# Last chunk of an attention stage reordered on TensorE, and place stores spread over two steps

## The chip, the cores and the metric

The kernel runs on one core of a Trainium2 chip. The metric is the device time of one execution in microseconds (us). Four runs of the kernel before took 470.43 to 471.54 us, with a median of 470.91 us.

The engines are named as in the profile: PE is the matrix engine (TensorE), PEld its weight loads, DVE the vector engine, ACT the scalar engine, POOL the GpSimd engine and SP the engine that only issues transfers. SBUF is the on-chip memory, PSUM the eight banks that PE writes its products to.

## The reference

Two blocks follow each other. The first is a linear attention with decay, on `q`, `k`, `v` of shape (4, 8, 768, 64): batch, heads, sequence, head dimension. Within a block of positions it is a masked product, and between blocks a state of 64 by 64 for each batch and head is carried on:

```python
for b in range(nb):
    intra = np.einsum('bhic,bhjc->bhij', qb, kb) * Dmask[None]
    intra = np.einsum('bhij,bhjd->bhid', intra, vb)
    inter = np.einsum('bhid,bhde->bhie', qb * lam_pow[None], kv_state)
    out[:, :, sl] = intra + inter
    kv_state = lam_block[None, :, None, None] * kv_state \
        + np.einsum('bhsd,bhse->bhde', kb * rev_pow[None], vb)
```

Its output, as 3072 tokens of 512 numbers, goes through a mixture of eight experts, each token to the one with the highest logit:

```python
logits = x @ w_gate                              # (3072, 512) @ (512, 8)
expert_idx = np.argmax(logits, axis=1)
...
h = np.maximum(xe @ w1[e], 0.0)                  # w1: (8, 512, 1024)
out[mask] = gate_w[mask, None] * (h @ w2[e])     # w2: (8, 1024, 512)
```

## The kernel before, in words

**Attention.** The sequence is cut into six chunks of 128 positions (n = 0 to 5). One step handles one chunk of two batches, so there are twelve steps, in the order (0; 0,1), (0; 2,3), (1; 0,1) and so on. In the code `cur` is the step's work, `last` the one before and `ahead` the one after. A step of the loop at line 710 does this:

- `leave(last)`: `rows` (lines 313 to 329) turns the finished output of the step before back into rows with matmuls into PSUM banks 4 to 7 (lines 319 and 321). Eight extra columns give the gate logits. ACT copies both out (325, 326) and writes the rows to `xs` in device memory. When the chunk's batches are complete, `choose` picks an expert for each token on DVE.
- `enter(ahead)`: loads for one chunk later are issued on SP; PE transposes q and k (line 207), and ACT and DVE copy them out.
- `attend_states(cur, 0)`, line 265: sixteen small matmuls, 64 by 64, of queries with the carried state, half of what the state gives. They write PSUM banks 6 and 7 (`op`). ACT then copies one element of the second bank to a tile called `fence` (line 273). The matmuls of `attend` that write that bank have to wait for this copy.
- `grow(cur)`, line 294: the state's increment. The last chunk has none.
- `attend(cur)`, line 277: the masked part, 32 matmuls of 128 by 64 into the same two banks.
- `attend_states(cur, 1)`: the other half of the state's part. Then `to_sbuf` (line 286) has ACT copy the two banks to the tiles `xT`, which `rows` reads in the next step, and `update` brings the state up to date.
- `give_places` for a chunk whose experts are chosen: `put` counts with two small matmuls into bank 5 (`rank`, line 375) which place a token takes on its expert's list, and computes its address on DVE (lines 384 to 389, result `slot_i`). One indirect transfer from POOL (line 391) for each batch then writes the tokens' entries to the lists in device memory, `slots`.
- `score(ahead)`, line 242: 32 matmuls of queries with keys for the next step. DVE multiplies them with the decays (line 248).

Chunks 0 to 4 have their places given once for all four batches, the last chunk once for each pair of batches. Chunk 3 is called `early`: when its places are stored, `start_early` (line 688) loads the first 256 places of expert 0 (`list_0a`), and POOL gathers those tokens from `xs` (`fetch`, line 437). After the loop, `turn(passes[0])` (line 466) transposes them on PE. Then come the places of the last chunk, with `leave` between its two pairs.

**Experts.** Eight experts follow in nine passes, since expert 0 is cut in two (0a and 0b). The first two passes multiply directly (lines 476 and 611). The later ones use seven products for eight (lines 552 and 580), for which POOL adds and subtracts blocks of the weights first (lines 513 and 516). Which expert comes first among the others is read back from the counts, so the lists and weights of the first pass after expert 0 are loaded on SP only after all places are stored (lines 413 and 174). Its tokens are gathered on POOL (line 437), partly behind the four sums of its first weights.

**What sets the order.** A planner orders each engine's instructions from estimated durations and readiness, and sets the semaphores. PE's matmuls of the attention stage, of `turn(passes[0])` and the counting matmuls of all but the last pair are pinned: on PE they stay in the order in which the program writes them. Matmuls of the passes, the small DVE work, ACT's copies and POOL's work are free, apart from what they depend on. Each engine then runs its own list strictly in order.

Of the kernel before, what the change touches and what calls it, by code (L numbers as in the profile page):

```python
# [10 lines left out]
F32 = mybir.dt.float32  # L11
# [10 lines left out]
def kernel(  # L22
# [29 lines left out]
    nc = tc.nc  # L52
# [4 lines left out]
    P = 128  # L57
    C = P
    NSTEP = S // C
    HP = H // 2  # L60
# [15 lines left out]
    const = ctx.enter_context(tc.tile_pool(name="const", bufs=1))  # L76
# [41 lines left out]
    nc.vector.memset(ones, 1.0)  # L118
    zeros = const.tile([P, P], F32, name="zeros")
    nc.vector.memset(zeros, 0.0)  # L120
    fence = const.tile([P, 1], F32, name="fence")

    nc.scalar.copy(fence, zeros[:, :1])

    rev = const.tile([P, E], F32, name="rev")
    nc.gpsimd.iota(rev, pattern=[[-1, E]], base=E, channel_multiplier=0,
# [15 lines left out]
    entry = const.tile([P, NSTEP, B, ENTRY], F32, name="entry")  # L142
# [46 lines left out]
    def bank(i, shape, name):  # L189
        return ps.tile(shape, F32, tag=f"bank{i}", name=name)  # L190
# [3 lines left out]
    halves = [slice(0, D), slice(D, P)]  # L194
# [3 lines left out]
    def pin(inst):  # L198
        tc.keep_in_program_order(inst)
# [37 lines left out]
    def score(m, s):  # L237

        shp = [P, HP // 2, 2, C]
        sp = [bank(2 * s + u, shp, f"sp{u}") for u in range(2)]  # L240
        for i, b, u in itertools.product(range(HP // 2), range(2), range(2)):
            pin(nc.tensor.matmul(  # L242
                sp[u][:, i, b, :], lhsT=m.kT[s][halves[u], i, b, :], rhs=m.qT[s][halves[u], i, b, :],
                start=(i == 0 and b == 0), stop=(i == HP // 2 - 1 and b == 1),
                skip_group_check=True))
        mt = work.tile([P, 2, HP // 2, 2, C], F32, tag="mt", name="mt")
        for u in range(2):
            nc.vector.tensor_mul(  # L248
                mt[:, u], sp[u],
                decay[:, u, s * HP // 2:(s + 1) * HP // 2].unsqueeze(2).to_broadcast(shp))  # L250
        m.mt.append(mt)
# [3 lines left out]
    def out_at(m, b, u, hp):  # L255
        return m.op[b][halves[u ^ (hp & 1)], hp, :]

    def attend_states(m, way):

        if way == 0:  # L260
            m.op = [bank(6 + b, [P, HP, C], f"op{b}") for b in range(2)]
        if m.n > 0:
            for hp, b in itertools.product(range(HP), range(2)):
                u = b ^ way
                pin(nc.tensor.matmul(  # L265
                    out_at(m, b, u, hp), lhsT=st[halves[u], m.b + b, hp, :],
                    rhs=m.qsT[hp // 2][halves[u], hp % 2, b, :],
                    start=(way == 0 and hp < 2), stop=(way == 1 and hp >= HP - 2),
                    skip_group_check=True))
        if m.n > 0 and way == 0:  # L270


            nc.scalar.copy(fence[halves[0]], out_at(m, 1, 1, HP - 1)[:, C - 1:])  # L273

    def attend(m):
        for hp, b, u in itertools.product(range(HP), range(2), range(2)):
            pin(nc.tensor.matmul(  # L277
                out_at(m, b, u, hp), lhsT=m.v[:, b, 2 * hp + u, :],
                rhs=m.mt[hp // 2][:, u, hp % 2, b, :],
                start=(m.n == 0 and hp == 0), stop=(m.n == 0 and hp == HP - 1),  # L280
                skip_group_check=True))

    def to_sbuf(m):
# [5 lines left out]
    def grow(m):  # L289

        if m.n < NSTEP - 1:
            m.cp = bank(4, [P, 2, HP, D], "cp")
            for hp, b, u in itertools.product(range(HP), range(2), range(2)):
                pin(nc.tensor.matmul(  # L294
                    m.cp[halves[u], b, hp, :],
                    lhsT=m.kd[hp // 2][:, b, 2 * (hp % 2) + u, :],
                    rhs=m.v[:, b, 2 * hp + u, :],
                    start=(hp == 0 and b == 0), stop=(hp == HP - 1 and b == 1),
                    skip_group_check=True))
# [68 lines left out]
    def put(n, bs, oh, ohc):  # L368


        nb = len(bs)
        shp = list(oh.shape)
        rank = bank(5, shp, "rank")
        for lhs, rhs in ((before, oh), (ones, ohc[:, :shp[1]])):
            mm = nc.tensor.matmul(rank, lhsT=lhs, rhs=rhs, start=(lhs is before),
                                  stop=(lhs is ones))

            if (n, bs[-1]) != (NSTEP - 1, B - 1):
                pin(mm)
        if shp[1] > nb:  # L380
            nc.vector.tensor_copy(had, rank[:, nb, 0:1])
        shp[1] = nb
        place = small.tile(shp, F32, tag="place", name="place")
        nc.vector.tensor_add(place, rank[:, :nb], base[0].unsqueeze(1).to_broadcast(shp))
        nc.vector.tensor_mul(place, place, oh[:, :nb])
        slot = small.tile([P, nb], F32, tag="slot", name="slot")
        nc.vector.reduce_sum(slot, place, axis=AX.X)
        slot_i = small.tile([P, nb], I32, tag="slot_i", name="slot_i")
        nc.vector.tensor_copy(slot_i, slot)  # L389
        for i, b in enumerate(bs):  # L390
            put = nc.gpsimd.indirect_dma_start(  # L391
                out=slots, out_offset=bass.IndirectOffsetOnAxis(ap=slot_i[:, i:i + 1], axis=0),
                in_=entry[:, n, b, :], in_offset=None)

            tc.declare_no_dep(put.ins, group="put", reason="disjoint rows of the lists")
            tc.add_to_no_dep_group("put", put.ins)

    empty = ffn.tile([P, E * R // P, ENTRY], I32, tag="xg", name="empty", bufs=2)
    nc.gpsimd.memset(empty, 0)
# [49 lines left out]
    def evac(i, dst, src):  # L449
        if i % 2:  # L450
            nc.scalar.copy(dst, src)
        else:
            nc.vector.tensor_copy(dst, src)  # L453
# [7 lines left out]
    def turn(m, pin=lambda inst: inst):  # L461
        m.xgT = ffn.tile([P, DC, m.n], F32, tag="xgT", name="xgT", bufs=1)
        for dc in range(DC):
            tp = bank(next(tp_banks), [P, m.n], "tp")
            for t, w in enumerate(m.widths):
                pin(nc.tensor.transpose(tp[:, t * P:t * P + w],  # L466
                                        m.xg[t // 2][:w, t % 2, dc * P:(dc + 1) * P],
                                        ident[:w, :w]))
            evac(dc, m.xgT[:, dc, :], tp)
# [178 lines left out]
    early = groups[NSTEP - 3]  # L648
# [16 lines left out]

    chosen = []

    def give_places(group):
        put(*group)
        if group[:2] == early:  # L670
            start_early()

    def leave(m):
        for b in range(2):
            n, bs = group_of[m.n, m.b + b]
            i = bs.index(m.b + b)
            if i == 0:
                lgs[0] = small.tile([P, len(bs), DC // 2, E], F32, tag="lg", name="lg")
            rows(m, b, lgs[0][:, i])
            if i == len(bs) - 1:  # L680

                chosen.append(choose(n, bs, lgs[0]))

    had = const.tile([P, 1], F32, name="had")
    passes = []
    skip = const.tile([P, 1], F32, name="skip")

    def start_early():

        nc.vector.tensor_scalar(out=skip, in0=had, scalar1=-1.0, scalar2=float(EARLY),  # L690
                                op0=ALU.mult, op1=ALU.add)
        nc.vector.tensor_scalar_max(skip, skip, 0.0)
        base[0] = const.tile([P, E], F32, name="ebase_late")
        nc.vector.tensor_copy(base[0], ebase)
        nc.vector.tensor_add(base[0][:, 0:1], base[0][:, 0:1], skip)
        m = make_pass(0, 0, EARLY, "0a")
        fetch(m, 1 + (NSTEP - 2) * B * C)
        passes.append(m)

    order = [(n, b) for n in range(NSTEP) for b in range(0, B, 2)]  # L700
    cur, last = enter(*order[0]), None
# [4 lines left out]
    for j, u in itertools.product(range(2), range(2)):  # L706
        pin(nc.scalar.dma_start(
            out=back[(u ^ j) * D:((u ^ j) + 1) * D, :, P + j * E:P + (j + 1) * E],
            in_=by_chunk[j, u]))
    for i in range(len(order)):  # L710
        due = chosen.pop() if chosen else None
        if last:
            leave(last)

        ahead = enter(*order[i + 1]) if 0 < i < len(order) - 1 else None
        attend_states(cur, 0)
        grow(cur)
        attend(cur)
        attend_states(cur, 1)
        to_sbuf(cur)  # L720
        if i == 0:
            ahead = enter(*order[1])
        update(cur)
        if i == 0:
            later_decays()

        if due:
            give_places(due)
        if i == 2:
            empty_lists()  # L730
        if ahead:
            for s in range(2):
                score(ahead, s)
        last, cur = cur, ahead
    turn(passes[0], pin)
    give_places(chosen.pop())
    leave(last)
    give_places(chosen.pop())


    cnt = bank(7, [P, E], "cnt")
# [19 lines left out]
                            op=ALU.is_equal)  # L761
# [55 lines left out]
    with tc.If(most > 0):  # L817
        for i in range(E):
            tiles = nc.values_load(beyond[0:1, i:i + 1], min_val=0, max_val=MORE[i])
            with tc.If(tiles > 0):  # L820
# [4 lines left out]
                with tc.For_i(0, tiles, 1) as r:  # L825
                    m = SimpleNamespace(n=P, widths=[P])
# [36 lines left out]
```

## Time and profile before

| | |
|---|---|
| median of four runs | 470.91 us (470.43 to 471.54) |
| the profiled execution | 470.12 us, of which the span is 468.2 us |
| granted TensorE clock in the span | 0.995 |
| attention, steps of the last chunk | about 110 to 131 us |
| first pass of expert 0 (line 476, line 611) | about 128 to 158 us |
| end of the first seven-product pass's gather | about 168 us |

All times inside an execution count from the span's start. A line of the order of time shows start, length, engine, line, operation, output and inputs, shape and count. In brackets stands how long the engine was idle before it and what ended that. PE's matmuls are pipelined: one of 270 ns may start every 37 to 62 ns, so the distance between starts, and not the length, tells the pace. "issue" as a releaser means that the profile shows nothing that the engine waited for.

### The profile page before, as it was taken

To read this page: it belongs to the slowest core of one execution; us is meant where nothing else is said; L and a number is where in the kernel's file an instruction comes from. 1 tells how busy PE (TensorE), PEld (TensorE's weight loads), DVE (VectorE), ACT (ScalarE), POOL (GpSimd) and SP (SyncE) were. 2 spreads that over 40 slices of the span, in tenths; PEclk is the share of its full clock that TensorE was granted. 3 is DMA by queue.
4 is the path that set the end of the run, shared out by engine and by line. 5 is a ranking of instruction groups with operands and counts; after the bars stand their busy time and mean duration, and the time that the engine had idled before them with its cause. 6 is when DMAs were issued, how large, how long until landed. Compare 5 with 4: busy or idle time off the path is not lost.

```text
span 468.2 us, 8613 instructions
## 1 busy us (share of the span) xinstructions
PE 449.5 (96%) x3447; PEld 373.3 (80%) x3447; DVE 222.0 (47%) x495; ACT 125.5 (27%) x323; POOL 246.9 (53%) x190
## 2 busy tenths in 40 slices
PE   5899999999899999999999999999999999999994
PEld 4789899998686667957994898699699689779863
DVE  3646859576550134452345437434524623753421
ACT  3454444554320111212121122113112212211210
POOL 5323636433163949859707951991695497711001
PEclk9999999999999999999999999999999999999998
DMA  9999999999317576060606152351624516001001
GB/s 178 228 259 255 221 245 230 243 264 357 95 48 275 179 262 221 25 251 30 224 1 247 48 203 109 138 202 49 244 92 155 231 34 224 1 20 45 1 18 52
DMA packets 99840, 72.60 MB, mean 155 GB/s; under 512 B 81235, under 2 KB 81239, under 8 KB 99792
## 3 DMA queue, kind: packets, MB, share of 16 engines
q1 hardware_dynamic: 90608, 52.49, 41.3%
q0 software_dynamic: 5008, 13.16, 7.8%
q10 hardware_dynamic: 4176, 6.31, 3.9%
q8 instruction: 29, 0.48, 0.5%
q14 instruction: 19, 0.16, 0.1%
HBM read 58.88 MB, written 13.16 MB: 154 GB/s over the span
## 4 chain that ended last, share of the span: by engine, by line
PE 62%; issue 4%; DMA 4%; POOL 4%; DVE 1%; SPq 0%; POOLq 0%; ACT 0%; DVEq 0%
PE p L552 27%; PE p L580 18%; PE po L611 14%; PE tp L466 3%; DMA w1t<-in_moe_w_dram 2%; POOL slots L391 1%; DMA slots<-entry,slot_i 1%; DMA xg<-xs,list 1%; POOL out_dram L443 1%; POOL s_k L516 1%; POOL w1t L513 1%; POOL s_q L516 1%; SPq L413 0%; DVE h_qsT L499 0%; POOL xg L437 0%
## 5 line engine op out<-in xcount | busy, mean ns | idle before, releaser
L611 PE MATMUL po<-w2t,hT 128*128 128x512 f32 (+5 forms) x224 | 81.0, 597 | 0.0
L437 POOL DMA_INDIRECT xg<-xs,list x24 | 25.8, 1075 | 70.2 <-PE tp L466 64.7
L611 PEld LDWEIGHTS po<-w2t,hT 128*128 128x128 f32 (+5 forms) x224 | 30.6, 162 | 38.2 <-issue 37.9
L563 ACT ACTIVATE hT<-hT 128x408 f32<-128x408 f32 (+4 forms) x56 | 29.5, 527 | 86.7 <-DVE hT L561 86.7
L443 POOL DMA_INDIRECT out_dram<-o,list x24 | 23.7, 989 | 50.9 <-DVE o L617 27.7
L552 PE MATMUL p<-xgT,w1t 128*128 128x204 f32 (+4 forms) x224 | 41.5, 329 | 0.0
L232 POOL TENSOR_TENSOR kd<-k_in,kdec 128x512 f32<-128x512 f32 x20 | 20.4, 1043 | 37.4 <-PE cp L294 23.5
L552 PEld LDWEIGHTS p<-xgT,w1t 128*128 128x128 f32 x224 | 37.6, 190 | 1.2 <-issue 0.9
L391 POOL DMA_INDIRECT slots<-entry,slot_i x24 | 23.3, 972 | 24.9 <-DVE slot_i L389 19.1
L248 DVE TENSOR_TENSOR mt<-sp,decay 128x512 f32<-128x512 f32 x48 | 29.8, 683 | 11.6 <-PE sp L242 11.4
L592 DVE SCALAR_TENSOR_TENSOR o<-p,list,o 128x256 f32<-128x256 f32 x28 | 13.6, 484 | 32.9 <-PE p L580 17.0
L580 PE MATMUL p<-w2t,hT 128*128 128x256 f32 x112 | 26.8, 382 | 0.0
L580 PEld LDWEIGHTS p<-w2t,hT 128*128 128x128 f32 x112 | 21.1, 190 | 7.0 <-issue 4.5
L242 PE MATMUL sp<-qT,kT 64*128 64x128 f32 x384 | 24.9, 279 | 0.0
L242 PEld LDWEIGHTS sp<-qT,kT 64*128 64x128 f32 x384 | 22.6, 188 | 1.8 <-issue 1.0
L277 PE MATMUL op<-mt,v_in 128*64 128x128 f32 x384 | 23.5, 274 | 0.2 <-ACT fence L273 0.2
L561 DVE TENSOR_TENSOR hT<-p,u_qsT 128x408 f32<-128x408 f32 (+4 forms) x28 | 15.7, 561 | 15.8 <-PE p L552 15.8
L466 PEld LDWEIGHTS tp<-ident,xg 128*128 128x128 f32 (+3 forms) x112 | 13.3, 140 | 11.9 <-issue 3.4
L476 PE MATMUL ph<-xgT,w1t 128*128 128x256 f32 (+1 forms) x128 | 22.5, 333 | 0.0
L286 ACT COPY xT<-op 128x512 f32<-128x512 f32 x24 | 12.9, 589 | 35.0 <-PE op L265 29.1
L277 PEld LDWEIGHTS op<-mt,v_in 128*64 128x64 f32 x384 | 20.7, 137 | 0.9 <-ACT fence L273 0.5
L466 PE MATMUL tp<-ident,xg 128*128 128x128 f32 (+3 forms) x112 | 18.6, 274 | 2.8 <-DVE xgT L453 1.4
(163 smaller groups left out, 934.5 us busy)
## 6 DMA issues: line engine op xcount, KB each, us to landing
w1t<-in_moe_w_dram SPq DMA_DIRECT2D x8, 2048.0 KB, 8.4
w2t<-in_moe_w_dram SPq DMA_DIRECT2D x8, 2048.0 KB, 8.5
v_in<-in_v_dram SPq DMA_DIRECT2D x12, 512.0 KB, 8.5
xs<-x ACTq DMA_DIRECT2D x24, 256.0 KB, 5.0
q_in<-in_q_dram SPq DMA_DIRECT2D x11, 512.0 KB, 8.2
k_in<-in_k_dram SPq DMA_DIRECT2D x11, 512.0 KB, 8.5
q_in<-in_q_dram SPq DMA_DIRECT2D x2, 256.0 KB, 3.8
k_in<-in_k_dram SPq DMA_DIRECT2D x2, 256.0 KB, 5.3
```

The costliest lines, as they stand in the source:

```text
L242: pin(nc.tensor.matmul(sp[u][:, i, b, :], lhsT=m.kT[s][halves[u], i, b, :], rhs=m.qT[s][halves[u], i, b, :], start=(i == 0 and b == 0), st ...
L248: nc.vector.tensor_mul(mt[:, u], sp[u], decay[:, u, s * HP // 2:(s + 1) * HP // 2].unsqueeze(2).to_broadcast(shp))
L277: pin(nc.tensor.matmul(out_at(m, b, u, hp), lhsT=m.v[:, b, 2 * hp + u, :], rhs=m.mt[hp // 2][:, u, hp % 2, b, :], start=(m.n == 0 and hp = ...
L391: put = nc.gpsimd.indirect_dma_start(out=slots, out_offset=bass.IndirectOffsetOnAxis(ap=slot_i[:, i:i + 1], axis=0), in_=entry[:, n, b, :] ...
L437: nc.gpsimd.indirect_dma_start(out=dst, out_offset=None, in_=xs[:rows, :], in_offset=bass.IndirectOffsetOnAxis(ap=idx, axis=0))
L443: put = nc.gpsimd.indirect_dma_start(out=out, out_offset=bass.IndirectOffsetOnAxis(ap=idx, axis=0), in_=src, in_offset=None, bounds_check= ...
L466: pin(nc.tensor.transpose(tp[:, t * P:t * P + w], m.xg[t // 2][:w, t % 2, dc * P:(dc + 1) * P], ident[:w, :w]))
L476: nc.tensor.matmul(ph, lhsT=w1t[:, dc, fc * P:(fc + 1) * P], rhs=m.xgT[:, dc, :], start=(dc == 0), stop=(dc == DC - 1))
L552: nc.tensor.matmul(p[:, i, :], lhsT=lhs[:, dc, (c + i) * P:(c + i + 1) * P], rhs=rhs[:, dc, :], start=(dc == 0), stop=(dc == DH - 1))
L563: nc.scalar.activation(outs[i][k], outs[i][k], ACT.Relu)
L580: nc.tensor.matmul(p, lhsT=lhs[:, fc, :], rhs=rhs[:, fc, :], start=(fc == 0), stop=(fc == FC // 2 - 1))
L611: nc.tensor.matmul(po[part], lhsT=m.hT[:, fc, t * P:t * P + w], rhs=w2t[:, fc, :], start=(i < k), stop=(i >= FC - k), skip_group_check=True)
```

## The change

For the last chunk (n = 5) alone, a step does the masked part `attend` first and then the states' first part, and the fence copy now reads two elements on all partitions. The scores of the next step come next, or in the very last step `turn(passes[0])`, and only then the states' second part. In all steps with states the second part takes batch 1 before batch 0. The stores of a chunk's places are no longer issued at once: `put` returns a function, `store_places` issues two of them in the step and two in the next one, and `start_early` comes when the early chunk's last store is issued.

```diff
-    fence = const.tile([P, 1], F32, name="fence")
-    nc.scalar.copy(fence, zeros[:, :1])
+    fence = const.tile([P, 2], F32, name="fence")
+    nc.scalar.copy(fence, zeros[:, :2])
...
+    def attend_begin(m):
+        m.op = [bank(6 + b, [P, HP, C], f"op{b}") for b in range(2)]
+
     def attend_states(m, way):
-        if way == 0:
-            m.op = [bank(6 + b, [P, HP, C], f"op{b}") for b in range(2)]
         if m.n > 0:
-            for hp, b in itertools.product(range(HP), range(2)):
+            for hp, b in itertools.product(range(HP), (0, 1) if way == 0 else (1, 0)):
                 u = b ^ way
                 pin(nc.tensor.matmul(
                     out_at(m, b, u, hp), lhsT=st[halves[u], m.b + b, hp, :],
                     rhs=m.qsT[hp // 2][halves[u], hp % 2, b, :],
-                    start=(way == 0 and hp < 2), stop=(way == 1 and hp >= HP - 2),
+                    start=(way == 0 and hp < 2 and m.n < NSTEP - 1),
+                    stop=(way == 1 and hp >= HP - 2),
                     skip_group_check=True))
         if m.n > 0 and way == 0:
-            nc.scalar.copy(fence[halves[0]], out_at(m, 1, 1, HP - 1)[:, C - 1:])
+            if m.n < NSTEP - 1:
+                nc.scalar.copy(fence[halves[0], :1], out_at(m, 1, 1, HP - 1)[:, C - 1:])
+            else:
+                nc.scalar.copy(fence, m.op[1][:, 0:HP:HP - 1, C - 1])
 
     def attend(m):
...
-                start=(m.n == 0 and hp == 0), stop=(m.n == 0 and hp == HP - 1),
+                start=(m.n in (0, NSTEP - 1) and hp == 0), stop=(m.n == 0 and hp == HP - 1),
...
-        for i, b in enumerate(bs):
+        def store(i):
             put = nc.gpsimd.indirect_dma_start(
                 out=slots, out_offset=bass.IndirectOffsetOnAxis(ap=slot_i[:, i:i + 1], axis=0),
-                in_=entry[:, n, b, :], in_offset=None)
+                in_=entry[:, n, bs[i], :], in_offset=None)
...
+        return store
...
+    waiting = []
+
+    def store_places():
+        for group, store, i in waiting:
+            for j in range(i, min(i + 2, len(group[1]))):
+                store(j)
+        done = [group for group, _, i in waiting if i + 2 >= len(group[1])]
+        waiting[:] = [(group, store, i + 2) for group, store, i in waiting
+                      if i + 2 < len(group[1])]
+        if any(group[:2] == early for group in done):
+            start_early()
+
     def give_places(group):
-        put(*group)
-        if group[:2] == early:
-            start_early()
+        waiting.append((group, put(*group), 0))
...
-        attend_states(cur, 0)
-        grow(cur)
-        attend(cur)
+        attend_begin(cur)
+        if cur.n < NSTEP - 1:
+            attend_states(cur, 0)
+            grow(cur)
+            attend(cur)
+        else:
+            attend(cur)
+            attend_states(cur, 0)
+            if ahead:
+                for s in range(2):
+                    score(ahead, s)
+            else:
+                turn(passes[0], pin)
         attend_states(cur, 1)
         to_sbuf(cur)
...
         if due:
             give_places(due)
+        store_places()
         if i == 2:
             empty_lists()
-        if ahead:
+        if ahead and cur.n < NSTEP - 1:
             for s in range(2):
                 score(ahead, s)
         last, cur = cur, ahead
-    turn(passes[0], pin)
     give_places(chosen.pop())
+    store_places()
     leave(last)
     give_places(chosen.pop())
+    store_places()
```

## The prediction

> **What bounds the kernel now.** I read the page's first table first, and then busy time by stage, for the stretch that the change rewrites and what follows:
>
> ```profile
> PE 449.5 (96%) x3447; PEld 373.3 (80%) x3447; DVE 222.0 (47%) x495; ACT 125.5 (27%) x323; POOL 246.9 (53%) x190
> ```
>
> ```profile
> 113.80:128.90 15.10, 13.00 (x190) 10.47 (x190) 8.16 (x34) 5.75 (x19) 3.06 (x4) 1.00 0.46 132
> 128.90:168.30 39.40, 39.10 (x192) 28.44 (x189) 9.03 (x45) 6.14 (x21) 24.67 (x20) 1.00 0.51 165
> 168.30:300.00 131.70, 131.70 (x644) 102.23 (x645) 59.75 (x105) 26.92 (x52) 86.61 (x51) 1.00 0.42 151
> ```
>
> PE is busy 96% of the 468.2 us span, so idle time of PE is what can move the end. In the stages the first pair is window and length, the next number PE's busy time. PE idles 2.10 us in the last chunk's two steps (113.8 to 128.9), 0.3 us in the 39 us after them, and nothing from 168.3 to 300. What PE loses before 168.3 the end loses. The third view is the order of time on all engines inside that stretch (start, length, engine, line):
>
> ```profile
> 114.39 0.44 PE L277 MATMUL op<-mt,v_in 128*64 128x128 f32 x4
> 115.05 1.75 PE L277 MATMUL op<-mt,v_in 128*64 128x128 f32 x28 [0.21 <-ACT fence L273]
> 117.44 1.08 ACT L286 COPY xT<-op 128x512 f32<-128x512 f32 x2 [2.45 <-PE op L265]
> 122.81 2.08 PE L277 MATMUL op<-mt,v_in 128*64 128x128 f32 x32
> 125.42 0.19 PE L375 MATMUL rank<-oh,before 128*128 128x32 bf16 x1
> 125.67 0.19 DVE L384 TENSOR_TENSOR place<-rank,ebase_late 128x32 f32<-128x32 f32 x1 [1.41 <-PE rank L375]
> 126.48 0.33 PE L466 MATMUL tp<-ident,xg 128*128 128x128 f32 x1 [0.84 <-DMA xg<-xs,list_0a]
> 127.48 0.42 DVE L453 COPY xgT<-tp 128x256 f32<-128x256 f32 x1 [1.54 <-PE tp L466]
> 127.82 0.18 DVE L385 TENSOR_TENSOR place<-place,oh 128x32 f32<-128x32 f32 x1
> 128.25 0.17 DVE L389 CAST slot_i<-slot 128x4 int32<-128x4 f32 x1
> 128.70 1.00 POOL L391 DMA_INDIRECT slots<-entry,slot_i  x1 [4.63 <-DVE slot_i L389]
> 128.94 0.48 PE L319 MATMUL tx<-back,xT 128*128 128x136 f32 x2
> ```
>
> To be seen: the fence costs something once, at 115.05; the first token tiles (xg of list_0a) land only at 126.48 and PE waits for them; chunk 4's list addresses (slot_i) are late because DVE stands at the evacuation of those tiles before it goes on with line 385. The chain that ended last says why that is not idle detail:
>
> ```profile
> 132.54 2.68 DMA slots<-entry,slot_i
> ...
> 137.59 2.08 DMA slots<-entry,slot_i
> ...
> 142.23 8.99 DMA w1t<-in_moe_w_dram
> ...
> 163.81 4.44 DMA xg<-xs,list
> 168.25 0.04 issue
> 168.29 1.17 PE tp L466 x6
> ```
>
> Eight stores of places run back to back on POOL from 128.70, 1.26 us apart (0.96 and 0.30 idle); the last one lands at 139.67; then come list loads, the second expert's w1 (landed 151.22), four sums of 2.35 us on POOL, two scatters, a gather, and PE, which is done with its own work at 168.02 (167.64 + 0.38), waits for that gather to 168.29. Two paths of the same length meet there: PE's own and the chain that begins with slot_i of chunk 4. The later one sets the end.
>
> **Part by part.**
>
> *Step for (5, batches 0 and 1).* Removed: the fence wait. States to scores took 5.51 us (113.80 to 119.31); without the wait the same work is 0.60 + 2.01 + 0.60 + 1.99 = 5.20 (attend from 122.81 to 124.82), so 0.31 is gained. Lost: the cover of the xT copies. Now 1.99 us of scores stand between the states' second part and the rows of line 319, which need xT; the two copies (1.08 us) hide in them. With the scores ahead of the second part, the rows follow it at once and wait for the first copy: 0.12 from the last start to ACT (117.32 to 117.44), 0.59 for one copy (row of line 286: 589 ns), 0.05 to PE, 0.76 in all. Net +0.45 us. The new fence (two elements on 128 partitions, one ACT copy like the old one at 158 ns) hides under the scores, which need nothing of it; were that cover gone it would cost the old 0.3.
>
> *Step for (5, batches 2 and 3).* Before, states, attend, states and rank run from 121.87 to 125.5. After: +0.45 at the start, the wait for the banks of the rows as before, attend and the first states to 125.15, then the turn of the first pass. Its data do not come earlier: the four stores of group 3 carry no new wait between them on POOL (no other POOL work lies between 109.93 and 114.73), the list load behind them left at 119.34, the gathers at 121.82 and 123.11. So the 0.45 is absorbed, and PE waits from 125.15 to 126.48, 1.33 us, for what cost it 0.95 before (125.53 to 126.48). The eight transposes with their evacuations last to 128.4, or to 128.8 with two of line 476's matmuls between them as now. Only then come the states' second part (0.60) and the rank of chunk 4: 129.0 to 129.4 instead of 125.42. Behind this rank on PE stand the rank of (5; 0,1) and the rows of (5; 2,3), and both wait: the second rank for the first place (line 384), the rows for xT, again uncovered. They start 0.76 after 129.0 to 129.4, at 129.8 to 130.2 instead of 128.94. PE path: +0.9 to +1.3; if the two matmuls of line 476 (0.42) are not inside the turn they come later, if two or three fill the new gap they give 0.4 to 0.6 back. I take +1.1, bounds +0.6 (the states' second part alone moved behind the gather) and +1.5.
>
> *The chain of places.* From rank to place 0.25 (125.42 to 125.67), from place to slot_i three steps of 0.21, from slot_i to the store 0.45: 1.32 after 129.0 to 129.4 is 130.3 to 130.7, against 128.70. So +1.6 to +2.0, although DVE's stand behind the evacuation (126.0 to 127.8) is gone. All eight stores follow back to back, since the last slot_i (135.34) had half a microsecond in hand and moves with them. Nothing later in the chain has slack before 168.25.
>
> *Stores two and two.* The same 24 stores. Those of groups 0 to 2 move past sd on POOL (for group 0: two at 51.1, two near 60.6 instead of 53.8) and kd of line 232 comes 2.5 us earlier (56.01 now); PE uses that kd at 64.91. Cost 0. If the cover were gone, a store costs POOL 1.26. The small DVE work that starts the early list moves one step later, ahead of base's next use at 125.67: 0. SP has nothing between its loads and the list load at 119.34, so what is moved past it costs nothing.
>
> *Order (1, 0) in the states' second part, in ten steps.* The trace has no such handover, so it is bounded: 0 from the scores' 1.98 us, which stand alike after states (38.47 to 40.46) and after attend (28.48 to 30.46); at best the longest matmul of line 265 (0.32 us) a step, 3.2 in all; at worst the 0.17 of idle that the weight loads show at a change of form, +1.7. I take 0, as the scores' row is the same handover with another predecessor.
>
> *Sum.* At 168.29: the larger of PE +1.1 less its 0.27 of wait, and the chain +1.85. End +1.85, on the profiled execution's 470.12 (span 468.2 and 1.9 around it): 471.97. That execution lies 0.79 under the median 470.91 of the runs; against the median it is 472.7 (rounded down from 472.76), which I give.
>
> **Two rules weighed.** PE already waits 0.84 us for xg at 126.48 in the row above. The Trainium skill, page "DMA: Bandwidth & Descriptors", section "Rules for kernel authors", advises to issue a DMA early and wait for it late, with compute in between; the change puts that wait ahead of 0.60 us of ready states. By that rule alone the sum would be +0.6.
> Weight loads idle 0.17 us at each change of form (125.42, "issue"). The page "TensorEngine Tiling (Array Packing)", section "Key Properties", says that changing the tiling mode drains TensorE. By it the last step's one further change of form would add 0.17; the row gives the same figure, but the starts of the scores show none of it on PE, so the sum goes without it.
>
> **Rivals.**
> *Filled gap.* The order on PE that is not pinned is the planner's. If it sees the late gather of 163.81 and puts matmuls of line 611 ahead of the transposes, the chain's delay hides behind them and PE's +1.1 remains: 471.2, against the median 472.0. For it: two of line 611 already stand between them at 169.39. Against: in the trace six transposes come first, though PE had to wait. 0.18.
> *Cancelled.* The early places land sooner: the row of their DMAs has 2.1 to 7.3 us to landing, the fourth early one took about 5.5 (113.77 to 119.3). At 2.1 the gather would be in by 123, the turn would begin at 125.15, rank of chunk 4 fall at 127.7, the store at 129.0: +0.3, or 471.2 against the median. Against: the change touches none of the traffic there. 0.08.
> *Faster.* The handover of the states' second part to the scores: in ten steps, gaining g each. It outweighs +1.85 from g = 0.19 on, and from 0.28 the gain passes 0.2% (0.94 us, about what a measurement of this kernel can tell from no change); at its bound of 0.32 the time is 470.9 + 1.85 - 3.2 = 469.6. Against it stands the equal 1.98. 0.10.
> *Worse.* The planner lets a sum (2.35 us) of POOL stand ahead of the gather at 163.81: +4.2, 475.1. For: from 151.36 to 166.0 POOL is never idle for more than 0.3 us, so nothing there would absorb it. 0.12.
>
> **How the numbers follow.** My forecast (chain late, +1.6 to +2.0, 472.5 to 472.9) has 0.52, filled gap 0.18, worse 0.12, faster 0.10, cancelled 0.08. Slower by over 0.2%: 0.52, the worse case's 0.12 and 0.10 of the filled gap (its bounds are 0.6 and 1.5, the line is 0.94): 0.74. Same: the other 0.08 of the filled gap and the cancelled case's 0.08: 0.16. Faster: 0.10. The range reaches down to 470.7, through the filled gap and most of the cancelled case, and up to 474.4, part of the way to the worse case; left out are the faster case and most of the worse one, 0.2.
>
> **What would show it.** Right: PE waits about 1.3 us for xg before line 466; the rank of chunk 4 behind these transposes, near 129.2; its first store near 130.5; a wait of 0.6 to 0.8 us of line 319 for xT near 119.1; a wait for xg near 168 to 170 of over 1 us. Wrong: the first store of chunk 4 before 129.5, or matmuls of line 611 ahead of the transposes at 168, or a different total of PE between 25 and 113.8, where I expect no change.

## The result, and the profile after

The changed kernel takes 473.44 us in the median of 52 runs (469.4 to 476.0), the kernel before, run beside it, 471.88 us in 78 (468.04 to 475.52). The ratio is 1.0032, with a 95% interval from 1.002 to 1.0044: slower by about 1.5 us. The profiled execution of the changed kernel took 474.02 us with a span of 472.2 us, 4.0 us longer than the span profiled before. A part of those 4.0 us belongs to that one execution, as will be seen. The page's first table shows PE busy for 2.8 us longer with the same 3447 matmuls:

```profile
PE 452.3 (96%) x3447; PEld 375.9 (80%) x3447; DVE 221.1 (47%) x495; ACT 125.7 (27%) x323; POOL 247.3 (52%) x190
```

The stages tell where. In these lines stand the window, its length, the busy time and count of PE, PEld, DVE, ACT and POOL, the granted clock of TensorE, the DMA share and GB/s:

```profile
113.80:128.90 15.10, 10.87 (x164) 8.88 (x160) 6.41 (x28) 4.19 (x15) 2.59 (x3) 0.96 0.41 116
128.90:168.30 39.40, 39.19 (x178) 27.60 (x178) 9.71 (x50) 6.74 (x21) 23.34 (x19) 0.93 0.45 151
...
124.00:126.00 2.00, 0.66 (x18) 0.42 (x16) 0.11 (x1) 0.16 (x1) 0.00 (x0) 1.00 0.82 272
126.00:128.00 2.00, 0.33 (x1) 0.14 (x1) 0.00 (x0) 0.00 (x0) 0.00 (x0) 0.95 0.20 80
128.00:130.00 2.00, 1.83 (x7) 1.14 (x7) 0.63 (x2) 0.37 (x1) 0.00 (x0) 0.50 0.00 0
130.00:132.00 2.00, 2.00 (x21) 1.44 (x21) 0.73 (x5) 1.06 (x3) 0.00 (x0) 0.50 0.00 0
132.00:134.00 2.00, 2.00 (x9) 1.57 (x7) 0.85 (x6) 0.39 (x1) 0.81 (x1) 0.50 0.00 0
134.00:136.00 2.00, 2.00 (x16) 2.00 (x15) 0.00 (x0) 0.94 (x5) 1.39 (x3) 0.84 0.02 1
```

Two things are to be seen. PE is busy 10.87 us of the last chunk's 15.10, where it was 13.00: the wait is there, and larger than forecast. And behind the wait TensorE's granted clock is halved for about 6.8 us, from 127.8 to 134.6, where the profile before shows 1.00. The order of time has both, with what they did to the places:

```profile
113.56 1.97 PE L282 MATMUL op<-mt,v_in 128*64 128x128 f32 x32
...
119.41 0.50 PE L324 MATMUL tx<-back,xT 128*128 128x136 f32 x2 [0.70 <-ACT xT L291]
...
124.00 0.67 PE L266 MATMUL op<-qsT,st 64*64 64x128 f32 x16
...
126.83 0.33 PE L474 MATMUL tp<-ident,xg 128*128 128x128 f32 x1 [2.16 <-DMA xg<-xs,list_0a]
128.08 2.11 PE L474 MATMUL tp<-ident,xg 128*128 128x128 f32 x7 [0.92 <-DMA xg<-xs,list_0a]
130.11 1.13 PE L266 MATMUL op<-qsT,st 64*64 64x128 f32 x16
131.18 0.21 PE L380 MATMUL rank<-oh,before 128*128 128x32 bf16 x1
...
132.74 0.17 DVE L394 CAST slot_i<-slot 128x4 int32<-128x4 f32 x1
133.19 1.00 POOL L396 DMA_INDIRECT slots<-entry,slot_i  x1 [9.50 <-DVE slot L392]
```

(The changed kernel's lines are shifted: 266 was 265, 282 was 277, 324 was 319, 380 was 375, 396 was 391, 474 was 466.) No fence wait is left at line 282. The rows of line 324 wait 0.70 us for xT. PE stands 2.16 us for the first token tile and 0.92 for the second, with one transpose between them. The sixteen state matmuls of line 266 that took 0.67 us at 124.00 take 1.13 at 130.11, which is the halved clock. The rank of chunk 4 comes at 131.18 instead of 125.42 and the first of the last eight stores at 133.19 instead of 128.70. The chain that ended last runs through the token gather and then stays on PE but for some 2 us on DVE from 136.87 (start, length, what):

```profile
122.73 5.30 DMA xg<-xs,list_0a
128.03 0.04 issue
128.08 0.49 PE tp L474
...
165.02 7.38 PE ph L484 x62
172.40 1.17 PE tp L474 x8
```

At 172.40 there is no wait for the gather, as there was one of 0.27 us at 168.29 before. In this execution PE itself, delayed by wait and clock, reached that point as late as the chain of places did.

### The profile page after: what moved, and what is told of

Its sections match the earlier page's. It is cut to its first block, busy times and chain, and to the rows that moved or that the text cites. A ratio compares the mean times of both kernels' runs of the same rounds, so it can differ in the third digit from the quotient of the medians.

```text
span 472.2 us, 8624 instructions
## 1 busy us (share of the span) xinstructions
PE 452.3 (96%) x3447; PEld 375.9 (80%) x3447; DVE 221.1 (47%) x495; ACT 125.7 (27%) x323; POOL 247.3 (52%) x190
## 4 chain that ended last, share of the span: by engine, by line
PE 70%; issue 2%; DVE 1%; DMA 1%; POOL 1%; POOLq 0%; ACT 0%
PE p L560 27%; PE p L588 18%; PE po L619 17%; PE ph L484 4%; PE tp L474 3%; DMA xg<-xs,list_0a 1%; POOL slots L396 0%; DVE h_qsT L507 0%; PE tx L324 0%; PE tx L326 0%; PE op L266 0%; DVE hT L569 0%; DVE xgT L461 0%; POOLq L848 0%; ACT hT L571 0%
## 5 line engine op out<-in xcount | busy, mean ns | idle before, releaser
L484 PE MATMUL ph<-xgT,w1t 128*128 128x256 f32 (+1 forms) x128 | 23.6, 342 | 0.0
```

Source lines behind the costliest of these rows:

```text
L484: nc.tensor.matmul(ph, lhsT=w1t[:, dc, fc * P:(fc + 1) * P], rhs=m.xgT[:, dc, :], start=(dc == 0), stop=(dc == DC - 1))
```

## The experiments

Two theories stood at the start. *Order*: the last step's order delays the rank, so the places, so the gather near 168, by about 1.9 us at full clock. *Clock*: PE's wait in the turn lets TensorE's granted clock fall to half, and that is the cost. A third question was whether the other parts cost anything. Twelve measurements were made in three comparisons, each with runs of the kernel before beside it. The median of the kernel before was 471.86 us (35 runs) in the first, 477.5 (30) in the second and 471.64 (35) in the third. In the second, attention ran 4 to 5 us later than in the profiles shown so far; what follows from that is told with it.

**The changed kernel with the last step as it was.**

```diff
-        if cur.n < NSTEP - 1:
+        cur.masked_first = cur.n == NSTEP - 1 and ahead is not None
+        if not cur.masked_first:
...
-            if ahead:
-                for s in range(2):
-                    score(ahead, s)
-            else:
-                turn(passes[0], pin)
+            for s in range(2):
+                score(ahead, s)
...
+    turn(passes[0], pin)
     give_places(chosen.pop())
```

> The changed kernel, but its very last step in the old order: states, masked part, states, rank of chunk 4, then the turn of the first pass. Everything else of the change stays (masked part first and scores between in the step for (5; 0,1), stores two and two, batch 1 before batch 0). Clock theory (PE idles some 3.4 us before the turn, its granted clock then halves for about 6 us): the wait for xg falls to 0.5 to 1.0 us, the granted clock of the span stays at 0.995 or more, the chunk-4 stores start within 0.3 us of the 128.7 of the kernel before, ratio to before 0.998 to 1.001. Order theory (chunk 4's places and the rows stand behind the gather, whatever the clock): the same ratio, 0.998 to 1.001. Rival that the loss is in the other parts (scores between, stores, batch order): ratio stays near 1.003.

Measured: 471.28 us, ratio 0.9986 (0.9957 to 1.0014). The loss is gone with the last step's order. The order of time of this kernel:

```profile
125.32 0.19 PE L380 MATMUL rank<-oh,before 128*128 128x32 bf16 x1
...
126.76 0.33 PE L474 MATMUL tp<-ident,xg 128*128 128x128 f32 x1 [1.23 <-DMA xg<-xs,list_0a]
...
129.06 1.00 POOL L396 DMA_INDIRECT slots<-entry,slot_i  x1 [4.68 <-DVE slot_i L394]
```

The rank is back at 125.32 and the first store at 129.06. It still holds the uncovered xT copy (0.71 us at line 324), the stores two and two and the order (1, 0): together they cost nothing that shows. Its span of 469.6 us has a halved clock too, from about 127.5 to 130.9.

**The last step's order alone, in the kernel before.**

```diff
-        attend_states(cur, 0)
-        grow(cur)
-        attend(cur)
+        attend_begin(cur)
+        cur.masked_first = ahead is None and i > 0
...
+            attend(cur)
+            attend_states(cur, 0)
+            turn(passes[0], pin)
         attend_states(cur, 1)
...
-    turn(passes[0], pin)
```

> The kernel before with the last step alone reordered as in the change: masked part, states' first part, turn of the first pass, states' second part (batch 1 first, in this step only). The step for (5; 0,1), the stores and the batch order elsewhere are as before. If the last step carries the loss: ratio to before 1.002 to 1.004, PE idle for 1.3 to 3.5 us before the turn, and the granted clock below 0.995 in a good part of the runs (clock theory) or 0.995 and more in all of them (order theory). If the other parts carry it: ratio 0.999 to 1.001.

Measured: 475.15 us, ratio 1.0071 (1.0045 to 1.0098). One part alone makes the loss, with the same picture: PE waits 1.87 and 0.68 us for xg, the clock is at 0.50 from about 126.6 to 133.4, the first store stands at 132.33. Why it lies above the whole change (1.0032) stays open. The intervals just miss each other, and the profiled span, 471.7 us, is not longer than the changed kernel's.

**The wait filled with matmuls.** Four matmuls of 128x512, whose result nobody reads, are added in front of the turn; nothing is left out.

```diff
             else:
+                busy = bank(2, [P, HP, C], "busy")
+                for j in range(4):
+                    pin(nc.tensor.matmul(busy, lhsT=ident, rhs=decay[:, 0], start=(j == 0),
+                                         stop=(j == 3)))
                 turn(passes[0], pin)
```

> The changed kernel with four matmuls of 128 by 512 put on PE between the last states' first part and the turn, where PE waits for xg. They read the identity and the decays into a bank that nobody reads, 0.43 us each by the row of line 611, so 1.7 us. The order and all waits stay. Clock theory: the idle stretch falls under 2 us, the granted clock stays at 0.995 or more in all runs, and the time falls by 1 us or more against the changed kernel: ratio to before 1.000 to 1.002. Order theory: ratio as for the changed kernel, 1.003, or up to 0.5 us more where the tokens land before the four matmuls are through.

Measured: 474.04 us, ratio 1.0048 (1.0024 to 1.0073), span of the profile 470.9 us. The clock stays at 1.00 in the profile, and 11 of the 12 runs have a mean granted clock of at least 0.9945, so filling the wait does keep it up. But the four took 3.70 us, not half of that, since each is carried out as two. The transposes began only at 128.07 and the first store left at 131.62, 0.7 us later than with two filling matmuls (130.94, see below). So the time settles nothing between the theories, and a run with two matmuls was needed.

**The turn behind the rows, in the kernel before.**

```diff
         last, cur = cur, ahead
-    turn(passes[0], pin)
     give_places(chosen.pop())
     leave(last)
+    turn(passes[0], pin)
     give_places(chosen.pop())
```

> The kernel before with one move in the other direction: the turn of the first pass stands on PE behind the rows of (5; 2,3) instead of ahead of the last chunk's first ranks. By the reading of the trace of before PE then has about 2 us of ready work while the tokens land (wait for xg 0 instead of 0.95 us), and chunk 4's slot_i no longer stands behind the evacuations on DVE (first store near 127.0 instead of 128.7). Both paths to 168.3 get shorter: PE by 0.9 to 1.3, the places by 1.5 or more: ratio to before 0.997 to 0.998. Rival: the turn's evacuations, now with nothing beside them, stall PE again as long: ratio 0.999 to 1.001.

Measured: 469.48 us, ratio 0.9954 (0.9932 to 0.9976). This is the change's step the other way round: rank and rows fill the time until the tokens are there. In a second set, in the third comparison, it gave 469.09 us, ratio 0.9965 (0.994 to 0.999):

> The kernel before with the turn of the first pass behind the rows, once more: 0.994 to 0.997 where PE of the kernel before waits for xg. Where it does not wait, PE gains nothing from the move, but the first store of chunk 4 still comes 1.5 us earlier, and the last pair's slot_i with it: 0.995 to 1.000. No run under a clock of 0.9945 in either regime (clock theory), or as many as for the kernel before (order theory).

Its order of time there:

```profile
125.69 0.19 PE L375 MATMUL rank<-oh,before 128*128 128x32 bf16 x1
...
127.28 1.00 POOL L391 DMA_INDIRECT slots<-entry,slot_i  x1 [2.19 <-DVE slot_i L389]
...
128.40 0.60 PE L466 MATMUL tp<-ident,xg 128*128 128x128 f32 x4
```

No wait for xg stands ahead of the transposes, the first store leaves at 127.28 though the rank is no earlier than before (125.69 to 125.42), since DVE has no evacuation in hand, and the clock is 1.00 in every window from 124 to 136. None of the twelve runs of either set has a mean granted clock below 0.9945 in its span; of the runs of the kernel before 20 and 21 of 35 have. It beats both kernels in these two comparisons; in the second one it was not run.

**The second comparison.** The changed kernel unaltered, with two filling matmuls instead of four (`range(2)` above), and two parts alone in the kernel before: the stores two and two, and the order of the states' second part.

```diff
-            for hp, b in itertools.product(range(HP), range(2)):
+            for hp, b in itertools.product(range(HP), (0, 1) if way == 0 else (1, 0)):
```

(the order alone; the stores alone are the `store`, `waiting` and `store_places` lines of the change)

> The changed kernel itself, beside the next three, so that they share the runs of the kernel before. Ratio 1.002 to 1.005. Of the kernel before 20 of 35 runs had a mean granted clock under 0.9945, of the changed one 39 of 54; clock theory: again more of the changed runs than of the runs before lie under 0.9945, and within one kernel those runs are 2 to 2.5 us longer. Order theory: the share of such runs does not differ.

> As the run with four filling matmuls, but with two. Four took 3.55 us (0.89 each, twice what was expected), and so held the turn up themselves; two take 1.78 and should end before the tokens land. Clock theory: idle stretches under 2 us, all or nearly all runs at 0.9945 or more, and the time 0.5 to 2 us under the changed kernel beside it: ratio 1.000 to 1.002. Order theory (places and rows behind the gather): ratio within 0.001 of the changed kernel's.

> The kernel before with the stores two and two and nothing else. Both theories: the places of chunks 0 to 3 are hidden and those of chunk 4 stay back to back, ratio 0.998 to 1.002, share of runs under a clock of 0.9945 as for the kernel before. Rival: the late pair delays the early list and with it the first tokens, ratio 1.002 or more.

> The kernel before with batch 1 ahead of batch 0 in the states' second part in all ten steps and nothing else. From the first states to the step for (5; 0,1) PE took 79.35 us in the kernel before and 79.07 in the changed one: ratio 0.998 to 1.002. Rival (a better or worse handover to the scores, up to 0.32 us a step better or 0.17 worse): ratio 0.993 to 0.997, or 1.002 to 1.004.

Measured: stores alone 477.08 us, ratio 0.9996 (0.9982 to 1.0011); order alone 476.95, ratio 0.999 (0.9976 to 1.0005). Both are nothing, as forecast. With two filling matmuls 476.88, ratio 0.9997 (0.998 to 1.0015). But the changed kernel was *faster* here: 475.21 us in 7 runs, ratio 0.9953 (0.9935 to 0.9971), where 1.002 to 1.005 was expected. A reason can be read from these profiles. All of them run later in attention: the rank of chunk 3 stands at 112.1 to 112.5, and at 107.9 in the third comparison's profile of the changed kernel. In that position the fence of step (5; 0,1) costs ten times as much. The kernel with the stores alone, a stand-in for the kernel before:

```profile
117.87 1.45 ACTq L329 DMA_DIRECT2D xs<-x  x1
...
120.51 0.59 ACT L226 COPY kT<-tk 128x512 f32<-128x512 f32 x1
120.99 0.16 ACT L273 COPY fence<-op 64x1 f32<-64x1 f32 x1
...
121.20 0.98 PE L277 MATMUL op<-mt,v_in 128*64 128x128 f32 x14 [1.98 <-ACT fence L273]
```

The fence copy stands last in ACT's queue, behind four copies of q and k, and these are late. Here ACT issues a write of rows in 1.45 us, which takes 0.33 in the kernel before (112.89). In the kernel with the order alone (fence wait 1.95 us) that issue takes 0.33 and ACT is idle for 0.86 us ahead of the second copy of q instead, for which the profile names only an instruction long done. Why ACT loses this time in that comparison is open. The changed kernel loses 0.84 us on ACT at the same place (ahead of 119.86), but its fence lies under the scores and no wait of PE for it is left. (Its masked part takes 2.42 us there, 117.99 to 120.41, instead of 1.89 in the first profile; the profile names no cause for that.) The rows that follow start at 124.36, against 125.46 in the kernel with the stores alone, and the spans are 472.5 and 473.9 us. When it comes to the turn the tokens have landed (order of time):

```profile
128.95 0.67 PE L266 MATMUL op<-qsT,st 64*64 64x128 f32 x16
129.55 0.66 PE L474 MATMUL tp<-ident,xg 128*128 128x128 f32 x4
```

No wait for xg, and the two filling matmuls, 1.98 us of PE, cost there what they are: the spans profiled are 474.5 and 472.5 us. So in these profiles the sign of the change goes with which of two waits an execution has. No run took the fence's wait away alone in that position, so for the gain this is read from traces and not shown by an experiment. What made attention late in that comparison was not tried. It is not the chip: the third comparison ran on the same one.

**The third comparison.** The changed kernel and the two filling matmuls once more.

> The changed kernel once more beside the kernel before. Two regimes were seen. Where PE comes to the last step before the first tokens have landed, it waits for them and the change costs (the measurement behind the prediction: 1.0032). Where the attention stage itself ran some 4.5 us later, the tokens were there, nothing waited, and the change gained (0.9953), most of it the fence, which had come to cost 2 us. Expected here: ratio 1.002 to 1.005 if the profile shows PE waiting over 1 us for xg, 0.994 to 0.997 if it shows no such wait. Rival: the sign does not go with that wait.

> The changed kernel with two filling matmuls (1.8 us) ahead of the turn. Where there was no wait for xg this cost 1.7 us against the changed kernel, as plain PE work. Where PE waits: clock theory: nearly all runs at 0.9945 or more where many of the changed kernel's are under it, and 0.5 to 2 us faster than the changed kernel beside it; order theory: within 0.5 us of it. Without a wait: again 1.5 to 2 us slower than the changed kernel.

Measured: changed 473.61 us, ratio 1.0038 (1.0013 to 1.0062), span 472.0; filled 473.31, ratio 1.0046 (1.002 to 1.0073), span 470.4. In the changed kernel the wait is 1.98 and 0.68 us, the clock goes to 0.50, and the first store leaves at 133.04. In the filled one:

```profile
124.47 1.98 PE L750 MATMUL busy<-decay,ident 128*128 128x512 f32 x4
...
126.81 0.33 PE L474 MATMUL tp<-ident,xg 128*128 128x128 f32 x1 [0.35 <-DMA xg<-xs,list_0a]
127.44 0.55 PE L474 MATMUL tp<-ident,xg 128*128 128x128 f32 x3 [0.30 <-DMA xg<-xs,list_0a]
...
129.47 0.19 PE L380 MATMUL rank<-oh,before 128*128 128x32 bf16 x1
...
130.94 1.00 POOL L396 DMA_INDIRECT slots<-entry,slot_i  x1 [6.76 <-DVE slot L392]
...
139.40 0.17 DVE L394 CAST slot_i<-slot 128x2 int32<-128x2 f32 x1 [3.10 <-DMA slots<-entry,slot_i]
139.84 0.96 POOL L396 DMA_INDIRECT slots<-entry,slot_i  x1 [1.58 <-DVE nth L793]
```

The last two lines show a second delay: the addresses of the last pair stand until an earlier store has landed, and the seventh of the eight stores leaves 1.58 us behind the sixth. In the changed kernel's first profile that gap is 0.75 us. In the kernel before it is the usual 0.30:

```profile
136.32 0.96 POOL L391 DMA_INDIRECT slots<-entry,slot_i  x1 [0.30 <-DVE both L764]
```

The windows of this profile show a clock of 1.00 throughout the stage; this is the change at full clock, and its span is 2.2 us longer than before's 468.2. So the last step's order costs time without the clock's help. That the cost runs through the places alone, as the *order* theory has it, is not shown: PE's own work ahead of 168 ends late as well, the first transposes there starting at 169.19 instead of 167.64, and then waits 0.30 and 0.41 us for the tokens. Keeping the clock up in 9 of 12 runs instead of 3 brought the median hardly nearer to before's (473.31 against 473.61), though the filling matmuls may cost something themselves. By the runs: those with a mean clock of at least 0.9945 have a median of 470.58 us in the kernel before (14 of 35), 471.69 in the changed one (3 of 12) and 472.78 in the filled one (9 of 12). The *clock* theory is right that the drop happens, and a mean clock below 0.9945 is found in more of the changed kernel's runs: in 39 of the 54 executions on record with the first result. But the kernel before has it as well in over half of its runs, so it explains little of the difference between the medians. An estimate: those 39 are 2.6 us longer in the median than the other 15 (474.02 against 471.38), and a share of 0.72 instead of 0.57 or 0.60 makes 0.3 to 0.4 us of the 1.5. Of the two profiled spans, 472.2 and 470.4, the 1.8 us between them go with the drop and with tokens that landed 0.64 us later.

**The first half of the change with the turn behind the rows.** The first experiment's kernel with the fourth's move.

```diff
     give_places(chosen.pop())
     store_places()
     leave(last)
+    turn(passes[0], pin)
     give_places(chosen.pop())
     store_places()
```

> The changed kernel with its very last step in the old order and the turn of the first pass behind the rows of (5; 2,3): no fence wait in the step for (5; 0,1), no work of the last chunk behind the tokens. Expected to beat both kernels in either regime: 0.994 to 0.997 where PE waits for xg (as the run with the turn moved alone, 0.9954), 0.992 to 0.996 where it does not (fence gone, chunk 4's places earlier). Rival: the uncovered xT copies (0.7 us) eat the fence's gain, and it is no faster than the run with the turn moved alone, beside it.

Measured: 470.47 us, ratio 0.9991 (0.9963 to 1.0019), so nothing over the kernel before, and behind the turn's move alone beside it (470.47 against 469.09 us in the medians; the two intervals overlap). One place where it loses shows in its order of time:

```profile
135.88 0.17 DVE L394 CAST slot_i<-slot 128x2 int32<-128x2 f32 x1 [3.90 <-DMA slots<-entry,slot_i]
...
136.32 0.96 POOL L396 DMA_INDIRECT slots<-entry,slot_i  x1 [1.87 <-DVE slot_i L394]
...
136.42 0.92 PE L484 MATMUL ph<-xgT,w1t 128*128 128x256 f32 x3 [1.13 <-DVE hT L467]
```

DVE may write the addresses of the last pair only when an earlier store that reads the same buffer has landed. It stands until 135.88, POOL stands 1.87 us for it, and PE 1.13 us for an evacuation (line 467) that is queued behind it on DVE. It is the delay of the seventh store met above. In the kernel with the turn's move alone the last stores leave back to back. Why the earlier store lands later in one kernel than in the other was not tried. The first store (127.13) is as early in both.

## Why the prediction was right, and where it was not

The forecast was 1.85 us more than before (472.7 against the 470.91 shown then). Measured were 1.5 us more by the ratio, and the time of 473.44 us lies inside the range. The direction holds, and so does the mechanism in its first half: PE waits for the tokens with ready work behind it, and the rank, the places and the rows come late. That the size came so near is partly luck. The sum lacked the halved clock, the second token tile's wait and the delay of the seventh store; the sign it gave for a late chain, a wait of over 1 us near 168, was not seen; and in the second comparison the same change was faster. By its steps:

- **Fence and xT copy, net +0.45.** Right in both terms. The fence wait is gone. The rows wait 0.70 us for xT, 0.76 were forecast. From the first matmul of the step to the rows it takes 5.85 us (113.56 to 119.41) instead of 5.51, so +0.34. It was absorbed as forecast: the kernel that has it without the last step's order (undo) is not slower.
- **PE's wait in the turn, 1.33 us.** Too small: 2.16 and 0.92 us in the profile after. The step had PE ready at 125.15 and the first tile there at 126.48. In the profile after PE is ready at 124.67 (0.48 earlier) and the first tile's transpose starts at 126.83 (0.35 later), so 1.33 became 2.16; the 0.92 for the second tile was not in the sum. Two more profiles have 1.98 and 0.68, and 1.87 and 0.68: the second tile is a transfer of its own, and its transposes start 0.6 to 1.3 us after the first one's. The trace of before showed this as a second wait of 0.30 us at 127.11; it lay inside the length taken for the turn, but was not counted as a wait that can grow.
- **Rank of chunk 4 at 129.0 to 129.4, first store at 130.3 to 130.7.** 129.47 and 130.94 in the profile with two filling matmuls, where the clock stays up: near the mark. Where the clock fell, 131.18 and 133.19. The 2.25 us between the two stores are 0.64 of later landing (128.08 against 127.44), 1.07 from there to the rank (3.10 against 2.03 us, half clock) and 0.54 from rank to store (2.01 against 1.47). In that last piece DVE takes the second rank's place (132.53) ahead of `slot_i` (132.74), and had to wait for that rank.
- **The chain sets the end, +1.85.** The size of the end stood, the path to it not quite. At full clock the span is 470.4, against the 470.05 that 468.2 and 1.85 give. The step had all eight stores back to back; the seventh left 3.52 us later than before (139.84 against 136.32), 2.24 of it from the first store and 1.28 from its own wait. The loads behind it gave a part back, and the gather near 168 is issued at 166.45 instead of 163.81, so 2.64 later. Nor was PE's own path +1.1: it came 1.55 later (169.19 against 167.64), with the filling matmuls in it. So the wait near 168, forecast as over 1 us, was 0.30 and 0.41 us there. In the profile after there was no such wait at all (172.24): PE, delayed by the clock, set the end.
- **Stores two and two at 0, order (1, 0) at 0.** Right: ratios of 0.9996 and 0.999. From the first states to step (5; 0,1) PE took 79.07 us, 79.35 before. The rival that needed 0.19 us for each handover is out.
- **Filled gap and worse.** Neither came. In the chain after eight transposes follow each other at 172.40, and no sum of POOL stands between the result writes and the gather at 167.92. Of the cancelled case only the early landing occurred, in the second comparison.
- **Not in the list.** The halved clock, and the executions in which the fence costs 2 us and the change gains 0.5%. The faster case named the handover; the wait that made it real was the fence, which the prediction had priced at 0.31 from its one row.

The two rules weighed came out like this. The Trainium skill, page "DMA: Bandwidth & Descriptors", section "Rules for kernel authors", says to issue early and wait late; with the turn behind the rows, so with the wait put later, the ratio is 0.9954 and 0.9965. The direction holds here. The +0.6 us worked out by it was only the states' second part; at full clock the span grew by 2.2 us, so that was only a part. For the 0.17 us at a change of tiling form, no run here shows any on PE.

## What to carry to other kernels

Before putting a wait earlier in an engine's queue, list what stands behind it. Here 3 us of waiting held up two tiny counting matmuls that eight serial stores, a list load and a gather 35 us later depended on, and PE's own later work with them. The same piece moved the other way, behind all work that was ready, gained 0.3 to 0.5% in the two comparisons in which it was run. And price a wait from more than one execution where it hangs on another engine's queue: the fence was worth 0.2 us in one set of runs and 2 us in another, and the sign of the change went with it.

## What the runs showed of the hardware

**The clock falls after short waits, too.** In the changed kernel with the last step as it was, three stretches of 3.4 us on both sides of the drop (windows, columns as above):

```profile
120.80:124.20 3.40, 2.96 (x47) 2.29 (x47) 1.78 (x11) 1.23 (x7) 1.77 (x2) 1.00 0.52 169
...
124.00:127.40 3.40, 1.87 (x36) 1.23 (x30) 0.27 (x2) 1.07 (x2) 0.37 (x1) 1.00 0.53 155
127.40:130.80 3.40, 3.31 (x14) 2.56 (x15) 1.68 (x8) 0.75 (x2) 1.44 (x2) 0.52 0.01 1
```

PE was busy for 1.87 us of the 3.4 before the drop, and the next 3.4 us ran at half clock. In the changed kernel PE was busy for 0.99 of the 3.4 us from 124.0, and 6.8 us ran at half. With two filling matmuls it was busy for 2.79 of these 3.4 us, and there was no drop. The Trainium skill, page "TensorE: Matmul & The Clock Gate", section "Part 1: The HAM clock gate", gives a free-running window of 3413 ns and half rate after at least one idle window. The stretches of about 3.4 and 6.8 us agree with that window; a wholly idle window was not needed here. The profile before, with 1.95 us busy in one such stretch, shows no drop:

```profile
125.40:128.80 3.40, 1.95 (x16) 1.31 (x13) 1.51 (x7) 1.45 (x3) 0.10 (x1) 1.00 0.14 53
```

So the busy time of a stretch laid anywhere does not decide it alone. That the same kernel has runs with a lower mean clock and runs without would fit a window that runs freely, but no run here shows where the window lies.

**A matmul of 128x512 in f32 is carried out as two.** Four of them appear as eight in the trace and took 3.70 us, two as four and 1.98 us, so 0.9 to 1.0 us each.
